# Regrouping sparse attention between feed-forward matmuls: two units of a set go through each stage together

## The chip, the cores and the metric

The kernel runs on one core of a Trainium2 chip. The core has five engines with instruction streams of their own: TensorE (PE in the profile, its weight loads PEld), VectorE (DVE), ScalarE (ACT), GpSimd (POOL) and SyncE (SP), which here issues DMAs. The metric is the device time of one execution in microseconds; lower is better. The median of three runs of the kernel before is 798.16 us (796.6 to 800.87).

## The reference

Block-sparse attention over 4 batches, 8 heads, 768 positions of 64 elements, followed by a feed-forward layer over all 3072 tokens. A query block of 32 positions sees its own key block and both neighbours, the first and the last block, and three sampled blocks; the first and the last query block see everything.

```python
scores = scale * np.matmul(q, k.transpose(0, 1, 3, 2))
mask = np.abs(blk_i - blk_j) <= window
mask = mask | (blk_i == 0) | (blk_j == 0) | (blk_i == n_blocks - 1) | (blk_j == n_blocks - 1)
...
scores = np.where(mask, scores, -1000000000.0)
scores = scores - np.max(scores, axis=-1, keepdims=True)
attn = np.exp(scores)
attn = attn / (np.sum(attn, axis=-1, keepdims=True) + 1e-09)
return np.matmul(attn, v).astype(np.float32)
...
h = x @ w_in
g = np.maximum(h, 0.0) + np.log1p(np.exp(-np.abs(h)))
return (g @ w_out).astype(np.float32)
```

Here x is the attention output with the heads side by side (512 columns), w_in is 512 x 2048, w_out 2048 x 512. Inputs and outputs are float32; the weights arrive as 64-bit words and are brought into float32 on the chip.

## The kernel before

**Attention.** A *set* is a batch and a group of four query blocks, with only the allowed key blocks (a sparse set), or the first and last query block of a batch against all keys (a *whole* set). A batch has seven sets: five sparse ones, the whole one, and one more sparse one of half the size; there are 28 in all. A set has two *units*, each with half of the heads. A unit goes through these functions:

- `scores` (line 606): matmuls into two PSUM banks (line 649 for sparse sets, 624 for the half-size one; 673 for the whole one, which takes two banks for each half of the keys, four in all), then on DVE a masked reduction that writes the scores to SBUF and their extremum (lines 655, 629, 680). For a sparse set these are four reductions.
- `exponents` (690): the exponential on ACT with its row sums (705), four per sparse unit.
- `transposes` (709): eight PE transposes of a sparse unit (718), four to a bank, so two banks; each bank is copied to SBUF by ACT (725) or DVE (723). In a set's first unit one copy goes to each of the two engines, in its second both go to ACT.
- `values` (730): small matmuls of the transposed weights with the values (761, 748, 775), all of a set into one bank of a pool of its own.

A set is ended by `normalise` (782, on DVE), `turn` (798: four PE transposes into one bank, tile y), `x_high` (817, ACT) and `x_low` (821, DVE). The last two read that bank and write the two parts of the feed-forward's input, and `x_low` of every third group stores them to DRAM.

**The feed-forward.** Each product of float32 matrices is made of three matmuls of high and low parts. In the first phase a *step* j treats one block of 128 hidden columns for a tile of 384 tokens: eight tiles by six blocks, 48 steps. In `first_half(j)` (292) stands `hidden` (248): twelve matmuls into one bank (lines 255 to 257, tile h), then ACT's absolute value and exponential (259, 260). In `second_half(j)` (297) stand `rounding` (263: 266 on ACT, 268 and 269 on DVE; 269 is the last reader of h's bank) and `project(j - 3)` (302): nine matmuls into three accumulators (313 to 315, tile o). ACT and DVE work of neighbouring steps (274, 279, 283, 289) completes the softplus. A second phase, after step 48, does the other ten blocks of hidden columns with tiles of 512 tokens and has no attention in it.

**PSUM.** Eight banks: three for o, one for x, and four of tag "s" (line 105), which h, s, t and y share.

**The order.** `pieces(n)` (828) makes three pieces out of unit n: `score_piece` (scores of unit n + 2), `value_piece` (exponents of n + 2, values of n) and `transpose_piece` (transposes of n + 1), with the ends of sets between them. 174 pieces stand in the list `attention` (918). `needs` (920) says how many must be done before the tile t of the feed-forward can start, and `due(x)` (950) spreads them evenly over the steps. The loop over j (973) emits `first_half(j)`, then pieces while fewer than `due(j + 0.5)` are done, then `second_half(j)`, then pieces up to `due(j + 1.0)`. In the steps 6 to 11, 18 to 23 and 30 to 35 this is three pieces, one unit, to a step; in the others about four. 22 pieces come before step 0. Pieces end at step 41.

`attend()` (924) runs one piece, then one `gather()` (477), which issues one waiting part of the key gathering (516 on DVE, 530 on POOL) and one of the value gathering (588, an indirect DMA on POOL), and one `convert()` (934), which advances the conversion of the weights (lines 160 to 206). Keys for the next group but one are requested by `load_keys` behind the second scores of a set, values by `load_values` behind its second values, queries by `load_queries` there too; the whole keys of the next batch are loaded (448) behind the last scores that read the old ones.

SP issues in the order of the program. On the other engines a planner at build time sets the order: it prefers the order of the program, and puts an instruction whose operands it takes to be ready ahead of one that has to wait. Instructions marked `keep_in_program_order` stay behind what precedes them on their engine.

## Time and profile before

| | us |
|---|---|
| median of three runs | 798.16 (796.6 to 800.87) |
| the profiled execution, its own time | 799.29 |
| its span in the profile | 797.5 |
| DVE e (268) waiting for ACT u (266), in total | 178.8 |
| ACT e (259) waiting for PE h (257), in total | 130.9 |
| POOL vg (588) waiting for PE x (761), in total | 38.6 |

The span runs from the first to the last instruction that the profiler saw; the profiled execution's time has 1.8 us more around it. Durations of single instructions come from that one execution. A matmul's row holds its whole passage through the array, and the rows of neighbours overlap; how far apart two rows start says what one costs. The page's chain of waits puts 66% of the span on PE, 16% on DVE and 11% on ACT. Most of the long totals in the table are idle time of engines that have nothing to do yet.

### The profile page before, as it was taken

To read this page: it belongs to the slowest core of one execution; us is meant where nothing else is said; L and a number is where in the kernel's file an instruction comes from. 1 tells how busy PE (TensorE), PEld (TensorE's weight loads), DVE (VectorE), ACT (ScalarE), POOL (GpSimd) and SP (SyncE) were. 2 spreads that over 40 slices of the span, in tenths; PEclk is the share of its full clock that TensorE was granted. 3 is DMA by queue.
4 is the path that set the end of the run, shared out by engine and by line. 5 is a ranking of instruction groups with operands and counts; after the bars stand their busy time and mean duration, and the time that the engine had idled before them with its cause. 6 is when DMAs were issued, how large, how long until landed. Compare 5 with 4: busy or idle time off the path is not lost.

```text
span 797.5 us, 20516 instructions
## 1 busy us (share of the span) xinstructions
PE 768.4 (96%) x7828; PEld 605.4 (76%) x7828; DVE 528.9 (66%) x1231; ACT 528.3 (66%) x1174; POOL 216.4 (27%) x389
## 2 busy tenths in 40 slices
PE   9779989998999999999999999999999999999997
PEld 8556667876777776787788888888888888888886
DVE  6789899787767878785656774555554553644544
ACT  5978978776777776777657875555555555555552
POOL 6874867425455435552000000000000000000000
PEclk9999999998999999999999999999999999999999
DMA  8999997876895886966415940330321312300201
GB/s 248 280 247 316 245 272 206 262 247 204 230 308 180 274 280 175 264 174 208 140 42 186 339 162 1 105 107 1 119 92 37 125 50 95 117 1 2 105 1 53
DMA packets 59729, 129.58 MB, mean 162 GB/s; under 512 B 5552, under 2 KB 17968, under 8 KB 58608
## 3 DMA queue, kind: packets, MB, share of 16 engines
q1 hardware_dynamic: 53632, 109.79, 44.5%
q0 software_dynamic: 5712, 17.57, 7.9%
q8 instruction: 61, 1.00, 0.5%
q10 hardware_dynamic: 288, 0.93, 0.3%
q14 instruction: 36, 0.29, 0.1%
HBM read 97.85 MB, written 30.41 MB: 161 GB/s over the span
## 4 chain that ended last, share of the span: by engine, by line
PE 66%; DVE 16%; ACT 11%; DMA 4%; issue 2%; SPq 0%; ACTq 0%; DVEq 0%
PE o L313 10%; PE o L314 10%; PE o L315 10%; PE h L255 9%; PE h L256 9%; PE h L257 9%; ACT pr L705 4%; PE t L718 2%; DVE pr L655 2%; DVE kg L516 2%; DMA vg<-in_v_dram 2%; PE x L761 2%; PE s L649 2%; DVE e L268 2%; DVE wt L183 1%
## 5 line engine op out<-in xcount | busy, mean ns | idle before, releaser
L268 DVE SCALAR_TENSOR_TENSOR e<-u,e 128x512 f32<-128x512 f32 (+1 forms) x108 | 76.7, 711 | 178.9 <-ACT u L266 178.8
L255 PE MATMUL h<-x,w 128*128 128x512 f32 (+1 forms) x432 | 163.2, 378 | 1.7 <-DVE e L269 0.9
L256 PE MATMUL h<-x,w 128*128 128x512 f32 (+1 forms) x432 | 159.3, 369 | 0.0
L257 PE MATMUL h<-x,w 128*128 128x512 f32 (+1 forms) x432 | 159.1, 368 | 0.0
L313 PE MATMUL o<-w,gh 128*128 128x512 f32 x384 | 156.5, 408 | 0.0
L314 PE MATMUL o<-w,gh 128*128 128x512 f32 x384 | 153.8, 401 | 0.0
L315 PE MATMUL o<-w,gl 128*128 128x512 f32 x384 | 152.1, 396 | 0.0
L259 ACT ACTIVATE e<-h 128x512 f32<-128x512 f32 (+1 forms) x108 | 59.3, 549 | 131.2 <-PE h L257 130.9
L705 ACT ACTIVATE pr<-pr,nmax 128x256 f32<-128x256 f32 (+1 forms) x192 | 102.2, 534 | 24.3 <-DVE nmax L686 12.0
L588 POOL DMA_INDIRECT vg<-in_v_dram,ix x88 | 87.6, 995 | 71.2 <-PE x L761 38.6
L255 PEld LDWEIGHTS h<-x,w 128*128 128x128 f32 x432 | 81.1, 188 | 19.3 <-DVE nmax L680 2.2
L530 POOL COPY kg<-kT 128x128 f32 x252 | 83.8, 378 | 39.4 <-PE s L649 31.2
L313 PEld LDWEIGHTS o<-w,gh 128*128 128x128 f32 x384 | 72.6, 189 | 24.4 <-issue 8.4
L283 ACT CAST gh<-u 128x512 fp32r<-128x512 f32 (+1 forms) x108 | 61.5, 569 | 43.5 <-PE o L314 41.0
L257 PEld LDWEIGHTS h<-x,w 128*128 128x128 f32 x432 | 81.2, 188 | 10.7
L256 PEld LDWEIGHTS h<-x,w 128*128 128x128 f32 x432 | 81.3, 188 | 10.6
L314 PEld LDWEIGHTS o<-w,gh 128*128 128x128 f32 x384 | 72.8, 190 | 17.6 <-issue 2.0
L315 PEld LDWEIGHTS o<-w,gl 128*128 128x128 f32 x384 | 72.6, 189 | 17.6 <-issue 0.4
L274 ACT ACTIVATE u<-u 128x512 f32<-128x512 f32 (+1 forms) x108 | 62.9, 583 | 23.2 <-DVE e L268 22.9
L289 DVE TENSOR_TENSOR gl<-u,gh 128x512 fp32r<-128x512 f32 (+1 forms) x108 | 69.4, 642 | 5.6 <-ACT gh L283 5.6
L279 DVE TENSOR_TENSOR u<-u,e 128x512 f32<-128x512 f32 (+1 forms) x108 | 69.6, 644 | 3.0 <-ACT u L274 1.6
L718 PE MATMUL t<-ident,pr 128*128 128x128 f32 x448 | 63.1, 280 | 7.9 <-DVE x L823 4.8
(88 smaller groups left out, 1060.4 us busy)
## 6 DMA issues: line engine op xcount, KB each, us to landing
vg<-in_v_dram SPq DMA_DIRECT2D x19, 768.0 KB, 6.7
xD<-x SPq DMA_DIRECT2D x8, 1536.0 KB, 8.3
raw<-in_w_in_dram SPq DMA_DIRECT2D x16, 512.0 KB, 9.2
raw<-in_w_out_dram SPq DMA_DIRECT2D x16, 512.0 KB, 8.8
qc<-in_q_dram SPq DMA_DIRECT2D x24, 256.0 KB, 6.9
vg<-in_v_dram SPq DMA_DIRECT2D x12, 512.0 KB, 7.2
yD<-os SPq DMA_DIRECT2D x24, 256.0 KB, 2.4
x<-xD SPq DMA_DIRECT2D x4, 1536.0 KB, 8.6
```

Of the source, the lines that this page charges most:

```text
L255: nc.tensor.matmul(ph, wh[:, cols], hi[:, c], start=(c == 0), stop=False)
L256: nc.tensor.matmul(ph, wh[:, cols], lo[:, c], start=False, stop=False)
L257: nc.tensor.matmul(ph, wl[:, cols], hi[:, c], start=False, stop=(c == NC - 1))
L268: nc.vector.scalar_tensor_tensor(out=e, in0=u, scalar=-1.0, in1=e, op0=ALU.add, op1=ALU.subtract)
L279: nc.vector.tensor_tensor(out=l, in0=l, in1=e, op=ALU.add)
L313: nc.tensor.matmul(po[m], gh[:, cols], wh, start=first, stop=False)
L314: nc.tensor.matmul(po[m], gh[:, cols], wl, start=False, stop=False)
L315: nc.tensor.matmul(po[m], gl[:, cols], wh, start=False, stop=last)
L530: copy(out=kd[:, i, 1 + NR + s, :], in_=kT[b][:, bass.ds(x, 1), :].rearrange("p n f -> p (n f)"))
L588: nc.gpsimd.indirect_dma_start(out=vd[0 : 3 * BLOCK, 1, i, :], out_offset=None, in_=v, in_offset=bass.IndirectOffsetOnAxis(ap=ix[:, b, 4 * ...
L705: nc.scalar.activation(x, x, AF.Exp, bias=nmax[rows, r, j : j + 1], scale=-1.0, accum_out=rs[rows, h : h + 1])
L718: nc.tensor.transpose(ps[:, i, 0:rows], st["pr"][r][0:rows, c * P : (c + 1) * P], ident[0:rows, 0:rows])
```

## The change

From set number 3 on (`SINGLE`), pieces are made for a whole set instead of for a unit. `set_pieces(k)` gives, for a sparse set followed by a sparse set, three pieces of count two: `scores_first` (`x_high` and `x_low` of the set before, then the scores of both units of the next set, and its key requests), `values_both` (exponents of both units of the next set, values of both units of this one, then the loads of values and queries) and `transposes_next` (`normalise`, transposes of both units of the next set, then `turn` of this one). `turn` stands directly behind `normalise` of the same set, where it came a unit later before. Around a whole set the pieces are cut differently, and both of its scores stand in neighbouring pieces.

The list `attention` now holds pairs of a count and a piece; `attend` adds the count to `done`, one by one, with a `gather` and a `convert` for each. The first loop, between `hidden` and `project`, does not run a `scores_first` unless attention is behind by more than `SLACK`. There are 169 units of count in place of 174 pieces, and 20 in place of 22 before step 0.

```diff
+SLACK = 2
+
+SINGLE = 3
...
+    def keys_behind(m):
+        b, g, whole = sets[m]
+        if not whole:
+            load_keys(place[b, g] + 2)
+        elif b + 1 < B:
+
+            gathered(key_work, place[b, g])
+            for n_ in range(4):
+                load_kT(b + 1, n_)
+            load_keys()
+
+    def set_pieces(k):
+
+        last = len(sets) - 1
+        nxt = k + 1 if k < last else None
+        out_ = []
+
+        def scores_first():
+            if k == SINGLE:
+                turn(k - 1)
+                transposes(2 * k + 1)
+            x_high(k - 1)
+            x_low(k - 1)
+            if nxt is not None:
+                scores(2 * nxt)
+                if not sets[nxt][2]:
+                    scores(2 * nxt + 1)
+                    keys_behind(nxt)
+
+        def scores_second():
+            exponents(2 * nxt)
+            scores(2 * nxt + 1)
+            keys_behind(nxt)
+
+        def exponents_next():
+            if nxt is not None:
+                if not sets[nxt][2]:
+                    exponents(2 * nxt)
+                exponents(2 * nxt + 1)
+
+        def behind_values():
+            load_values(k + 2)
+            if nxt is not None and not sets[nxt][2]:
+                load_queries(place[sets[nxt][:2]] + 2)
+
+        def values_first():
+            values(2 * k)
+            transposes(2 * k + 1)
+
+        def values_second():
+            exponents_next()
+            values(2 * k + 1)
+            behind_values()
+
+        def values_both():
+            exponents_next()
+            values(2 * k)
+            values(2 * k + 1)
+            behind_values()
+
+        def transposes_next():
+            normalise(k)
+            if nxt is not None:
+                transposes(2 * nxt)
+                if not sets[nxt][2]:
+                    transposes(2 * nxt + 1)
+            turn(k)
+
+        def split_last():
+            x_high(k)
+            x_low(k)
+
+        if sets[k][2]:
+            out_ += [(1, values_first), (2, scores_first), (1, values_second)]
+        elif nxt is not None and sets[nxt][2]:
+            out_ += [(1, scores_first), (1, scores_second), (2, values_both)]
+        else:
+            out_ += [(2, scores_first), (2, values_both)]
+        out_.append((2, transposes_next))
+        if nxt is None:
+            out_.append((1, split_last))
+        return out_
...
-    attention = [piece for n in range(len(units) + 2) for piece in pieces(n)]
-
-    needs = [3 * sum(1 for m, a in units if place[sets[m][:2]] < (t + 1) * GROUPS) + 4 for t in range(NTB)]
-    needs[-1] = len(attention)
+    attention = [(1, piece) for n in range(2 * SINGLE) for piece in pieces(n)]
+    split_in = {m: 3 * (2 * m + 3) + 1 for m in range(SINGLE - 1)}
+    for k_ in range(SINGLE, len(sets)):
+        split_in[k_ - 1] = sum(c for c, _ in attention) + (3 if sets[k_][2] else 2)
+        attention += set_pieces(k_)
+
+    total = sum(c for c, _ in attention)
+    needs = [
+        split_in[max(m for m, x in enumerate(sets) if place[x[:2]] < (t + 1) * GROUPS)] for t in range(NTB - 1)
+    ] + [total]
     done = 0
 
     def attend():
         nonlocal done
-        attention[done]()
-        done += 1
-        gather()
-        convert()
+        cost, piece = attention.pop(0)
+        piece()
+        for _ in range(cost):
+            done += 1
+            gather()
+            convert()
...
-        while done < len(attention) and done < due(j + 0.5):
+        while attention and done < due(j + 0.5) and (
+            attention[0][1].__name__ != "scores_first" or done + SLACK < due(j + 0.5)
+        ):
             attend()
...
-        while done < len(attention) and done < due(j + 1.0):
+        while attention and done < due(j + 1.0):
             attend()
```

More of the change, by code (lines that the diff above doesn't have):

```diff
@@ L957, in due @@
             last, at = end, needs[t]
-        return len(attention)
+        return total
     def load_w2(f):
@@ L990, in sparse_attention_ffn @@
         second_half(j)
-        while done < len(attention) and done < due(j + 1.0):
+        while attention and done < due(j + 1.0):
             attend()
         convert()
-        if done == len(attention) and ahead is None:
+        if not attention and ahead is None:
             assert weights.done(), weights.at
```

## The prediction

> **What bounds the kernel now.** I read the page's head first, then the busy time by stage, then the instructions in order of time inside one stage. The head says that TensorE (PE) is nearly always busy:
>
> ```profile
> span 797.5 us, 20516 instructions
> PE 768.4 (96%) x7828; PEld 605.4 (76%) x7828; DVE 528.9 (66%) x1231; ACT 528.3 (66%) x1174; POOL 216.4 (27%) x389
> ```
>
> That average mixes stages, so I cut the span where step 0, 6, 12, 18, 24, 30 and 36 of the first phase begins, and where attention has run out (stretch, length, then busy us and count of PE, PEld, DVE, ACT, POOL, granted clock, DMA share, GB/s):
>
> ```profile
> 57.08:119.74 62.66, 57.13 (x862) 40.66 (x855) 58.92 (x149) 53.67 (x133) 40.55 (x66) 0.97 0.99 279
> 119.74:166.50 46.76, 46.42 (x765) 36.97 (x763) 39.43 (x107) 37.31 (x99) 25.64 (x38) 1.00 0.76 239
> 166.50:228.71 62.21, 58.12 (x813) 43.46 (x812) 48.03 (x125) 45.34 (x115) 29.60 (x62) 0.95 0.79 238
> 228.71:276.53 47.82, 46.92 (x764) 37.08 (x763) 36.75 (x103) 37.19 (x101) 24.33 (x36) 1.00 0.77 237
> 276.53:335.38 58.85, 56.01 (x812) 42.26 (x811) 47.04 (x121) 43.74 (x111) 29.59 (x62) 1.00 0.84 244
> 335.38:384.54 49.16, 48.97 (x781) 37.77 (x779) 37.06 (x104) 35.20 (x97) 20.21 (x33) 1.00 0.64 190
> 421.65:446.87 25.22, 25.22 (x128) 22.78 (x127) 19.48 (x37) 20.55 (x43) 0.00 (x0) 1.00 0.70 245
> ```
>
> Steps 0 to 5 are bound by VectorE (58.92 of 62.66 us, 94%). From step 6 PE is the bound (46.42 of 46.76), with DVE at 84% and ACT at 80%. From there on whatever shortens PE's stream shortens the kernel, unless DVE or ACT are then asked for something sooner than they can give it.
>
> Now PE's stream inside one step, in order of time (start, duration, engine, line, operation). h is `hidden`, s `scores`, o `project`, x `values`, t `transposes`:
>
> ```profile
> 228.73 0.42 PE L255 MATMUL h<-x,w 128*128 128x384 f32 x1
> ...
> 230.73 0.34 PE L257 MATMUL h<-x,w 128*128 128x384 f32 x1
> 230.99 1.09 PE L649 MATMUL s<-kg,qc 64*32 64x256 f32 x32
> 232.02 0.50 PE L313 MATMUL o<-w,gh 128*128 128x512 f32 x1
> 232.36 0.39 PE L314 MATMUL o<-w,gh 128*128 128x512 f32 x1
> 232.59 0.40 PE L315 MATMUL o<-w,gl 128*128 128x512 f32 x1
> ...
> 234.76 1.10 PE L761 MATMUL x<-vg,pt 128*32 128x64 f32 x64
> 235.79 1.09 PE L718 MATMUL t<-ident,pr 128*128 128x128 f32 x8
> ```
>
> and where later steps begin, the last two without attention:
>
> ```profile
> 244.12 0.42 PE L255 MATMUL h<-x,w 128*128 128x384 f32 x1
> 426.08 0.34 PE L255 MATMUL h<-x,w 128*128 128x384 f32 x1
> ...
> 430.30 0.34 PE L255 MATMUL h<-x,w 128*128 128x384 f32 x1
> ```
>
> Two steps with two units, which is one set, take 244.12 - 228.73 = 15.39 us. A step without attention takes 430.30 - 426.08 = 4.22. So a set costs PE 15.39 - 2 x 4.22 = 6.95 us. How much of that is work? Inside s, eight weight loads fall into each stretch of 0.21 to 0.22 us, one per matmul, so 32 are four such waves, 0.86 us; x and t take what their weight loads take:
>
> ```profile
> 231.23:231.45 0.22, 0.22 (x16) 0.15 (x8) 1.00 1.02 261
> 231.45:231.66 0.21, 0.21 (x16) 0.15 (x8) 1.00 0.76 215
> 234.76 0.94 PEld L761 LDWEIGHTS x<-vg,pt 128*32 128x32 f32 x64 [0.17 <-DMA qc<-in_q_dram]
> 235.79 0.86 PEld L718 LDWEIGHTS t<-ident,pr 128*128 128x128 f32 x8
> ```
>
> I take 0.86 + 0.90 + 0.86 = 2.62 per unit, and 0.43 for the four transposes of `turn` (half of the eight): 2 x 2.62 + 0.43 = 5.67. The other 6.95 - 5.67 = 1.28 us are borders between kinds of matmul. They can be seen singly: s begins 0.26 after the last h; the first o begins 1.03 after s although s is 0.86 of work; the first o takes 0.34 where the next takes 0.23. Before, two steps hold ten such borders (h-s, s-o, o-x, x-t, t-h, twice; `turn` stands in front of x): 0.13 each.
>
> **The change part by part.** From `due()` I worked out which piece falls into which half step. All seven needs shift by 2 (22 becomes 20, 46 becomes 44 and so on; 174 pieces become 169 units of count), so the pace by step and the end of attention (step 41) stay. In the steps with three units of count (6 to 11, 18 to 23, 30 to 35) two steps become: h, both t with y, o, both s | h, o, both x. Borders: h-t, y-o, o-s, s-h, o-x, x-h: six for ten.
>
> Gain: 4 x 0.13 = 0.51 us a set. Counted by islands of attention among h and o it is three for four at 1.28 / 4 = 0.32 each, so 0.32; both are bounds from the same rows, and I take 0.5, since it is the borders that show in the rows. Twenty sparse sets get paired scores (24 less the first four). Four of them fall before step 6, where DVE is the bound, and get nothing. 16 x 0.5 = **-8 us**.
>
> Loss 1, PSUM banks. Tag "s" has four. Both t take four, y a fifth, and in those nine sets h still holds one: six for four. The nearest sight is step 17, where h, one t (two banks) and s (two) want five (PE, then ACT, then DVE):
>
> ```profile
> 219.24 0.44 PE L255 MATMUL h<-x,w 128*128 128x384 f32 x1
> ...
> 221.43 1.03 PE L718 MATMUL t<-ident,pr 128*128 128x128 f32 x8
> 222.40 2.23 PE L649 MATMUL s<-kg,qc 64*32 64x256 f32 x32
> 224.56 0.49 PE L313 MATMUL o<-w,gh 128*128 128x512 f32 x1
> 222.94 1.05 ACT L725 COPY pt<-t 128x512 f32<-128x512 f32 x2
> 224.45 0.56 DVE L268 SCALAR_TENSOR_TENSOR e<-u,e 128x384 f32<-128x384 f32 x1 [3.09 <-ACT u L266]
> 225.04 0.56 DVE L269 SCALAR_TENSOR_TENSOR e<-h,e 128x384 f32<-128x384 f32 x1
> ```
>
> s lasts 2.16 us to the next o instead of 1.03: 1.13 us lost until the copy of t gives a bank back; h's own bank comes only with L269, 6.4 us after h began. In the new order the second t tile is copied by DVE beside ACT, so I expect the fourth t to wait about 0.6 us (first t done 2.7 us after h starts, two activations of h and one copy of 0.53 before the bank is free, against a demand at 3.4). The program order is only a preference: an instruction whose operands are ready may be put ahead, so an o can fill the wait. I take 0.35, ends 0 and 1.13: 9 x 0.35 = **+3 us**.
>
> Loss 2, whole sets. Their two scores now follow each other with four banks each, in three batches behind step 6. Reducing 256 columns goes at this pitch:
>
> ```profile
> 233.55 0.42 DVE L655 CUSTOM_DVE_ANT_1 pr<-s,mask 128x256 f32<-128x256 f32 x1
> 233.90 0.42 DVE L655 CUSTOM_DVE_ANT_1 pr<-s,mask 128x256 f32<-128x256 f32 x1
> ```
>
> 0.35 us, so 384 columns about 0.5 (estimate) and four of them 2 us: the second unit waits between 0 and 2 us. I take 0.5: **+1.5 us**.
>
> Gain 2: at steps 17 and 29 the crowding just shown goes, since h is now followed by o: about -1.1 each. What is late next there: the transposes one step on need eight exponents at 0.53 us each, 4.3 us:
>
> ```profile
> L705 ACT ACTIVATE pr<-pr,nmax 128x256 f32<-128x256 f32 (+1 forms) x192 | 102.2, 534 | 24.3 <-DVE nmax L686 12.0
> ```
>
> between the pair of scores and the pair of transposes, which there lie x (1.9) and h (2.1), 4 us, apart. That may give half of it back: **-2 us** kept over the three crowded stretches, ends -3.5 and +2.
>
> Costed at nothing: the DMAs. Value loads (L570 and L582 on SP, L588 on POOL) are issued behind the second unit of a set as before, and used one pair later instead of three units later, so they have more time. Query loads stand behind them on SP in the same order. Key gathering (L516 on DVE, L530 on POOL) follows the second score as before; it stands behind eight reductions instead of four, and its user is two pairs away. The weight conversion gets two ticks in a row after a piece of count two; same work, burstier. If DVE's cover of 16% is not enough, L516 and L183 stand before the reductions that h needs, and each is a wait of 0.7 to 1.1 us. The start: a value and an exponent of set 3 move behind the first h, which begins 1 to 2 us sooner, but into the stretch that DVE bounds: 0, ends -2 and 0.
>
> Sum against the profiled run's own 799.29 us: -8 + 3 + 1.5 - 2 = -5.5, about **793.8 us**. The median of the runs shown, 798.16, lies 1.1 below the profiled one, so a median may come out 1 us lower.
>
> **The rivals.**
>
> *The banks give it all back.* If each of the sixteen pairs waits 0.5 us somewhere (the fourth t, or h behind both s, which fill all four banks), the sum is 0 and the time stays at 798 to 800. For it: four banks, and pairs that want all of them. Against: no wait at all in steps 6 to 11 today. The same time comes out if the pairs are pulled apart again because one half is ready sooner, so that the change doesn't do what it says. Together 0.31.
>
> *Slower: h behind the pair of scores.* s, s, h want five banks, and h gets its bank only when DVE has done the first unit's two reductions. If DVE is then in anything else, PE stands, and h, the head of the long chain h, three activations, L268, L269, starts late and the next demand on the banks with it. Its price is the 1.13 us of step 17, once per pair: 16 x (1.13 - 0.5) = +10, 809 us; it decides when the wait per pair passes 0.5 us. For it: DVE at 84%, one copy or conversion is 0.7 us. Against: the reductions of the first unit can run while PE does the second's 0.86. 0.21. [...]
>
> *Faster: the long waits go as well.* The clock was 0.97 and 0.95 in two stretches: 0.03 x 62.66 + 0.05 x 62.21 = 5.0 us lost. In the second, this piece of the chain of waits stands beside POOL's copies:
>
> ```profile
> 187.74 5.88 DVE kg L516
> 187.23 4.33 POOL L530 COPY kg<-kT 128x128 f32 x18
> ```
>
> If coarser pieces move those copies apart and PE does not pause, the clock stays whole: 793.8 - 5 = 789, and 3 us more without the DVE stall: 786. Against: the batch change keeps its place, steps 12 to 14. 0.14. [...]
>
> **How the numbers follow.** Forecast 0.34, all given back 0.31, slower 0.21, long waits gone 0.14. A measurement of this kernel can tell 0.5%, 4 us. The forecast, 5.5 us, lies just beyond that, and its own range (gain a set 0.32 to 0.51, banks 0 to 1.13) runs from 787 to 801; nearly all of its chance counts as faster. Faster 0.47, same 0.32, slower 0.21. The range reaches from the fast rival to most of the slow one: 784 to 807.
>
> **What would show it.** Right: between steps 6 and 11 two steps take about 14.9 to 15.3 us instead of 15.39, with x64, x64 and s32, s32 adjacent on PE. Loss 1 right: waits of PE t on ACT or DVE copies behind h, a few tenths each. Wrong: h waiting on L655 by more than 0.5 us per pair, PE busy well under 98% from step 6 on, or steps 0 to 5 longer than 62.7 us because bursts on DVE cannot be carried.

## The result and the profile after

| | before | after |
|---|---|---|
| median, us | 799.21 (796.6 to 800.87, 4 runs) | 809.13 (808.15 to 809.94, 4 runs) |
| ratio, 95% interval | | 1.0127 [1.0094, 1.0159] |
| the profiled execution, own time / span, us | 799.29 / 797.5 | 808.85 / 807.1 |
| start of step 0, of step 6, us | 57.08, 119.74 | 59.37, 129.63 |
| from step 6 to the end, us | 677.76 | 677.47 |

The change makes the kernel slower by 10 us, 1.3%. The forecast was 793.8, the range 784 to 807; 809 is the number of the slow rival. In the profile of after, lines up to 877 have moved by 4: L259 is the former L255, L653 is L649, L659 is L655, L722 is L718, L765 is L761, L273 is L269, L827 is L823.

The head of the page of after, and the longest of TensorE's waits (us in total, times, longest):

```profile
PE 762.3 (94%) x7828; PEld 614.6 (76%) x7828; DVE 521.0 (65%) x1231; ACT 527.6 (65%) x1174; POOL 218.4 (27%) x389
```

```profile
PE h L259 <- DVE nmax L659: 10.4, 9, 2.2
```

TensorE is busy for 6 us less than before (762.3 against 768.4, with as many matmuls) and yet ends 10 us later. The first matmul of `hidden` waits nine times, 10.4 us in all, for the reduction of the scores.

The same cuts as before, at the steps 0, 6, 12, 18, 24 and 30 of after and where attention has run out (stretch, length, busy us and count of PE, PEld, DVE, ACT, POOL, granted clock, DMA share, GB/s):

```profile
59.37:129.63 70.26, 60.23 (x911) 44.74 (x911) 60.29 (x155) 55.16 (x141) 42.02 (x67) 0.85 0.83 246
129.63:178.61 48.98, 45.70 (x766) 37.54 (x762) 38.44 (x103) 37.20 (x101) 24.39 (x36) 1.00 0.72 228
178.61:234.52 55.91, 52.98 (x818) 42.10 (x811) 42.59 (x121) 41.69 (x102) 29.19 (x59) 1.00 0.86 256
234.52:283.63 49.11, 45.04 (x767) 37.58 (x763) 38.03 (x106) 39.04 (x109) 24.62 (x38) 1.00 0.78 232
283.63:343.94 60.31, 54.54 (x817) 43.56 (x811) 44.24 (x123) 44.29 (x110) 31.54 (x62) 0.97 0.81 241
343.94:435.52 91.58, 90.05 (x1303) 75.22 (x1300) 57.03 (x161) 61.68 (x155) 21.45 (x34) 0.98 0.46 143
```

Against 62.66, 46.76, 62.21, 47.82, 58.85 and 90.47 us before (the last is 49.16 + 41.31, steps 30 to 41) that is +7.6, +2.2, -6.3, +1.3, +1.5 and +1.1. So in this pair of profiles the whole loss lies ahead of step 6 (2.3 us before step 0, 7.6 in steps 0 to 5). Behind it, gains and losses cancel. 64 values have moved from ahead of step 0 into steps 0 to 5 (880 matmuls ahead of step 0 instead of 944), and yet step 0 begins later. VectorE, which filled 94% of steps 0 to 5 before, fills 86% of them now: with about the same work (60.29 us in 155 instructions against 58.92 in 149) it is made to wait.

**Behind step 6.** TensorE's matmuls of step 6 in after, in order of time:

```profile
131.84 1.47 PE L722 MATMUL t<-ident,pr 128*128 128x128 f32 x12
133.07 0.48 PE L317 MATMUL o<-w,gh 128*128 128x512 f32 x1
133.61 0.66 PE L722 MATMUL t<-ident,pr 128*128 128x128 f32 x4
...
136.51 2.70 PE L653 MATMUL s<-kg,qc 64*32 64x256 f32 x64
140.43 0.41 PE L259 MATMUL h<-x,w 128*128 128x384 f32 x1 [1.23 <-DVE nmax L659]
```

and VectorE's instructions in the same stretch:

```profile
135.55 1.45 DVE L174 TENSOR_SCALAR wt<-wt 128x512 f32<-128x512 f32 x1 [0.38 <-ACT wt L164]
...
138.90 0.69 DVE L187 SCALAR_TENSOR_TENSOR wt<-raw,wt 128x512 int32<-128x512 int32 x1
139.51 0.42 DVE L659 CUSTOM_DVE_ANT_1 pr<-s,mask 128x256 f32<-128x256 f32 x1
...
139.85 0.42 DVE L659 CUSTOM_DVE_ANT_1 pr<-s,mask 128x256 f32<-128x256 f32 x1
```

Two things are to be seen. The fourth tile of transposes comes later than the third, and one matmul of `project` fills the gap (t x12, o, t x4); that it lacks a bank is what the other two profiles of this kernel say, in which it waits 0.7 us for ACT's copy of a tile t. And the pair of scores, which starts at 136.51, finds VectorE in three conversions of weights (L174, L181, L187) and three other instructions until 139.51. Only after two reductions does h get its bank: 3.92 us from s to h. Where VectorE is free, at step 32, the same order runs without a stall:

```profile
361.35 0.44 PE L259 MATMUL h<-x,w 128*128 128x384 f32 x1
...
368.20 1.96 PE L653 MATMUL s<-kg,qc 64*32 64x256 f32 x64
370.31 0.41 PE L259 MATMUL h<-x,w 128*128 128x384 f32 x1 [0.15 <-PE s L653]
...
376.59 0.44 PE L259 MATMUL h<-x,w 128*128 128x384 f32 x1
```

Here s to h takes 2.11, and two steps 376.59 - 361.35 = 15.24 us, against 15.39 before.

**Ahead of step 6.** TensorE's waits in the steps 0 to 5 of after (us in total, times, longest):

```profile
PE s L653 <- DVE e L273: 3.3, 1, 3.3
PE h L259 <- DVE nmax L659: 2.2, 1, 2.2
PE s L628 <- POOL kg L534: 2.1, 1, 2.1
```

Before, the longest in that stretch was one of 3.0, and the next 0.7. The first of the new ones in TensorE's order of time:

```profile
119.41 1.48 PE L653 MATMUL s<-kg,qc 64*32 64x256 f32 x34
124.18 1.95 PE L653 MATMUL s<-kg,qc 64*32 64x256 f32 x30 [3.29 <-DVE e L273]
```

Half of the scores run, then the pair wants a bank that h still holds: L273, the last reader of h, stands on VectorE behind 4 us of weight conversion, softplus and `normalise`. The granted clock falls as well, to 0.50 from 123.00 to 129.63 (0.85 over the steps 0 to 5), and the 128 values then take 3.64 us, where they take 1.99 at step 33 at a whole clock.

The second of the waits is that of the first matmul of step 0, and so lies ahead of that step. TensorE and VectorE in after:

```profile
54.47 2.70 PE L653 MATMUL s<-kg,qc 64*32 64x256 f32 x64
59.40 0.41 PE L259 MATMUL h<-x,w 128*128 128x384 f32 x1 [2.22 <-DVE nmax L659]
56.31 0.43 DVE L174 TENSOR_SCALAR wt<-wt 128x512 f32<-128x512 f32 x1
56.77 1.80 DVE L181 TENSOR_SCALAR wt<-wt 128x512 int32<-128x512 int32 x1
58.49 0.41 DVE L659 CUSTOM_DVE_ANT_1 pr<-s,mask 128x256 f32<-128x256 f32 x1
```

and in the kernel "scores apart" below (chip 2), whose matmuls stand in the same order there:

```profile
54.72 2.70 PE L653 MATMUL s<-kg,qc 64*32 64x256 f32 x64
57.58 0.41 PE L259 MATMUL h<-x,w 128*128 128x384 f32 x1 [0.16 <-PE s L653]
56.65 0.42 DVE L659 CUSTOM_DVE_ANT_1 pr<-s,mask 128x256 f32<-128x256 f32 x1
```

In after, two conversions of weights stand on VectorE ahead of the reductions; there, the reductions come first. The second conversion takes 1.80 us, where the median of its line is 0.43: GpSimd's own part of the conversion (L191) runs from 56.97 to 58.27, and so it does from 135.38 to 136.70, beside the L174 of 1.45 us in step 6. No run moved L191 alone.

### The profile page after: what moved, and what is told of

Same layout as the page of the kernel before. It is cut to its first block, busy times and chain, and to the rows that moved or that the text cites. A ratio compares the mean times of both kernels' runs of the same rounds, so it can differ in the third digit from the quotient of the medians.

```text
span 807.1 us, 20545 instructions
## 1 busy us (share of the span) xinstructions
PE 762.3 (94%) x7828; PEld 614.6 (76%) x7828; DVE 521.0 (65%) x1231; ACT 527.6 (65%) x1174; POOL 218.4 (27%) x389
## 3 DMA queue, kind: packets, MB, share of 16 engines
q8 instruction: 62, 1.02, 0.5%
## 4 chain that ended last, share of the span: by engine, by line
PE 76%; ACT 9%; DVE 8%; issue 3%; DMA 2%; POOL 0%; SPq 0%; DVEq 0%; POOLq 0%; ACTq 0%
PE h L259 11%; PE h L260 11%; PE h L261 11%; PE o L318 10%; PE o L317 10%; PE o L319 10%; PE x L765 4%; ACT pr L709 2%; PE t L722 2%; PE s L653 2%; ACT pt L729 2%; PE s L677 2%; PE warm L980 2%; ACT e L263 1%; DVE pr L659 1%
## 5 line engine op out<-in xcount | busy, mean ns | idle before, releaser
L272 DVE SCALAR_TENSOR_TENSOR e<-u,e 128x512 f32<-128x512 f32 (+1 forms) x108 | 72.4, 670 | 178.1 <-ACT u L270 177.7
L259 PE MATMUL h<-x,w 128*128 128x512 f32 (+1 forms) x432 | 165.5, 383 | 11.2 <-DVE nmax L659 10.4
L260 PE MATMUL h<-x,w 128*128 128x512 f32 (+1 forms) x432 | 161.8, 375 | 0.0
L261 PE MATMUL h<-x,w 128*128 128x512 f32 (+1 forms) x432 | 161.4, 374 | 0.0
L259 PEld LDWEIGHTS h<-x,w 128*128 128x128 f32 x432 | 82.8, 192 | 33.6 <-PE s L653 10.1
L261 PEld LDWEIGHTS h<-x,w 128*128 128x128 f32 x432 | 83.2, 193 | 10.7
L260 PEld LDWEIGHTS h<-x,w 128*128 128x128 f32 x432 | 83.0, 192 | 10.5
L293 DVE TENSOR_TENSOR gl<-u,gh 128x512 fp32r<-128x512 f32 (+1 forms) x108 | 72.3, 669 | 5.0 <-ACT gh L287 5.0
L273 DVE SCALAR_TENSOR_TENSOR e<-h,e 128x512 f32<-128x512 f32 (+1 forms) x108 | 67.9, 629 | 2.6
```

Source lines behind the costliest of these rows:

```text
L259: nc.tensor.matmul(ph, wh[:, cols], hi[:, c], start=(c == 0), stop=False)
L260: nc.tensor.matmul(ph, wh[:, cols], lo[:, c], start=False, stop=False)
L261: nc.tensor.matmul(ph, wl[:, cols], hi[:, c], start=False, stop=(c == NC - 1))
L272: nc.vector.scalar_tensor_tensor(out=e, in0=u, scalar=-1.0, in1=e, op0=ALU.add, op1=ALU.subtract)
L293: nc.vector.tensor_tensor(out=gl, in0=l, in1=G[n].bitcast(F32), op=ALU.subtract)
```

## The experiments

All ratios are to the kernel before, run beside it on the same chip. On two chips (5 and 2 below) the kernel before took 800 us, as in the result; on three others (9, 1 and 3) it took 811 to 812. There almost everything came out level; the end of this part says what is known of the reason. So the first four runs are to be read beside the later ones.

**Sets 3 to 8 unit by unit** (chip 9).

```diff
-SINGLE = 3
+SINGLE = 9
```

> Sets 3 to 8 go unit by unit as before, pairs begin with set 9 (step 6 on). Theory A (the loss arises before step 6: pairs there make PE pause, the granted clock falls to half for some 20 us, and later gains and waits of pairs cancel): the start of step 6 comes about 10 us earlier than in the changed kernel, the mean clock is back near 0.99, time about 799. Theory B (every pair loses the same by waits behind its scores; the low clock is by the way): 14 of 20 pairs are left, so about 0.7 of the 10 us, time about 806.

0.9994 [0.997, 1.0017]: level.

**Scores apart.** The two scores of a set in separate pieces, except behind a whole set; values and transposes still in pairs (chip 9).

```diff
-                if not sets[nxt][2]:
+                if sets[k][2]:
                     scores(2 * nxt + 1)
...
-        elif nxt is not None and sets[nxt][2]:
+        elif nxt is not None:
             out_ += [(1, scores_first), (1, scores_second), (2, values_both)]
```

> Values and transposes stay in pairs, but the two scores of a set are pieces of their own again. Theory A (the four banks that a pair of scores takes at once meet a DVE queue that still holds other work): the waits behind s64 go (about 14 us summed over the trace) and most of the half clock before step 6 (8 us), one more island a set costs 20 x 0.3 = 6 us: about 793. Theory B (the pairs of transposes, or the doubled ticks of weight conversion, make the bursts): 805 or more.

0.9949 [0.9915, 0.9982]. Steps 6 to 11 take 46.9 us and steps 18 to 23 47.6, as before the change: the waits of h are nearly gone (1.5 us in two, 10.4 in nine in after). Steps 0 to 5 still take 71.8.

What the edit does is not the same everywhere. In the steps with three units of count the two scores then stand apart on TensorE, with matmuls of the feed-forward between them. In the steps 0 to 5, and in the other steps with about four units, they still follow each other directly or with some values between (64 in one row at 54.72 us above); what changes there is the order on the other engines.

**No conversion behind the scores.** The ticks of weight conversion behind `scores_first` are made up for behind the next pieces (chip 9).

```diff
+    late = 0
...
+            if piece.__name__ == "scores_first":
+                late += 1
+                continue
             convert()
+            if late:
+                late -= 1
+                convert()
```

> The changed kernel, but scores_first is followed by no weight conversion; its ticks are made up behind later pieces. Theory C (conversion work traced right around the pair of scores stands before x_low and the reductions on DVE): the waits behind s64 in steps 6 to 11 fall from 0.6 to 1.8 us to under 0.3, time 4 to 8 us shorter, 801 to 805. Theory A without C (any DVE work will do, the planner fills the queue anyway): within 2 us of 809.

0.9973 [0.9948, 0.9999]; steps 6 to 11 at 50.3, steps 0 to 5 at 70.3. The waits of h are 4.5 us in five, against 9.9 in nine in the next run, on the same chip. So the conversion is part of what stands in the way, and not all of it: behind step 6 waits of 0.6 to 1.5 us are left.

**Without the rule of SLACK** (chip 9).

```diff
-        while attention and done < due(j + 0.5) and (
-            attention[0][1].__name__ != "scores_first" or done + SLACK < due(j + 0.5)
-        ):
+        while attention and done < due(j + 0.5):
```

> The changed kernel without the rule that a pair of scores waits for the projection. If the bank that h holds behind hidden matters, the pairs of scores that now stand between h and o wait for L269 (about 4 us behind h's end): 1 us or more for each of some 9 pairs, 815 to 825. If the place does not matter: within 2 us of 809.

1.0018 [0.9984, 1.0052]: no effect that can be told.

**Both kernels again** (chip 5), with a second profile of the kernel before.

> The changed kernel once more, beside many runs of the kernel before on the same chip, since four runs of each gave 799 against 809 on one chip and the kernel before took 812 on another. Theory D (the start of the kernel, up to step 6, depends on the chip and hides the difference where the kernel before also pauses there): ratio between 0.995 and 1.005 where the kernel before takes over 808, about 1.01 where it takes about 800. Theory A (pairs cost a fixed 10 us): ratio 1.010 to 1.015 on any chip.

> The kernel before, for a profile on the same chip. Theory D: where it takes over 808, the time is lost before step 6 (step 6 later than at 125 us, against 119.7 in the first profile), with half clock there; steps 6 to 41 take the same 306 us within 3.

1.0167 [1.0144, 1.0191]: the loss is there again, and somewhat larger. In this pair of profiles step 6 begins at 127.14 instead of 119.26 us, 7.9 later, step 12 at 178.81 instead of 165.99, 12.8 later, and the span is 12.8 longer (807.9 against 795.1). In the first pair step 12 was 12.1 later (178.61 against 166.50). So in both the whole loss is there by step 12; how it divides at step 6 differs.

**Values apart.** `values_both` as two pieces, scores and transposes in pairs (chip 5).

```diff
...
-            out_ += [(2, scores_first), (2, values_both)]
+            out_ += [(2, scores_first), (1, values_one), (1, values_two)]
...
```

> Scores and transposes in pairs, the two values of a set as pieces of their own. Theory E (128 values in a row after 64 scores run through PE's instructions faster than they are fetched: the pause of 2.9 us inside the values of step 29): that pause and the half clock behind it go, 4 to 5 us less than the changed kernel, but one more island a set, 20 x 0.3 = 6 us: about the same time as the changed kernel, or 3 us more. If the pause stays, it is not the row of values that makes it.

1.0131 [1.0107, 1.0155], 2.9 us less than after beside it (809.38 against 812.31). On TensorE the values still stand in rows of 128 (at 143.95 and 175.87, for example). So the edit did not take them apart, and what their pairs cost was not measured. The pause in the values of step 29 is still there, 2.8 us.

**Sets 3 to 8 unit by unit and all scores apart**, the first two edits together (chip 5).

> Both of e1 and e2: sets 3 to 8 unit by unit, and from set 9 on values and transposes in pairs, scores apart. Theory A or D with waits behind the pair of scores: steps 0 to 5 as in the kernel before, steps 6 to 41 without waits behind scores and with 0.3 to 0.5 us less a set than before, 14 x 0.35 = 5 us: ratio to the kernel before 0.993 to 0.996. Theory B: 1.000 or more.

0.9967 [0.9953, 0.998]: the whole loss is gone and a little more: 0.3% less than the kernel before. But which of the two edits does it?

**The square** (chip 2): after, each of the two edits alone, and both, beside each other.

> The changed kernel once more, as one corner of a square whose other corners run beside it on the same chip: sets 3 to 8 taken as pairs or not, and the two scores of a set adjacent or apart. Theory A (two separate losses that add): 1.3 to 1.7% over the kernel before, as seen so far. Theory B (one loss, the scores): the same.

> Sets 3 to 8 unit by unit, later scores in pairs. Theory A (pairs in the stretch that VectorE bounds cost 7 us up to step 6, adjacent scores behind it cost about 6 more): steps 0 to 5 back at 62 to 64 us, steps 6 to 11 at 49 to 50, and half of the loss left: 1.005 to 1.009. Theory B (adjacent scores are the whole loss, wherever they are): 1.008 to 1.013, since three quarters of the pairs are left.

> All sets from set 3 on with values and transposes in pairs, scores always apart. Theory A: steps 0 to 5 still 68 to 72 us, steps 6 to 11 at 47, and half of the loss left: 1.005 to 1.009. Theory B: no loss left, 0.995 to 1.000, with steps 0 to 5 at 62 to 64 us.

> Both edits together. Theory A: both losses gone, 0.995 to 0.999, steps 0 to 5 at 63 us and steps 6 to 11 at 47. Theory B: the same as with scores apart alone.

| | sets 3 to 8 in pairs | sets 3 to 8 unit by unit |
|---|---|---|
| scores in one piece | 1.0128 [1.0106, 1.015], 809.8 us | 1.0004 [0.9989, 1.0018], 799.55 us |
| scores in two pieces | 0.9994 [0.9981, 1.0007], 799.58 us | 0.9969 [0.9952, 0.9985], 797.29 us |

Both theories fell. Each edit alone takes 10 us off, both together 12.5. Two losses that add would have left half with either edit; adjacent scores alone, at one price per set, would have left most of it in the right upper corner. So nearly 8 us need both at once: sets 3 to 8 in pairs, and the scores of a set in one piece. The windows say where: steps 0 to 5 and steps 6 to 11, first after, then unit by unit, then scores apart, then both, and last the kernel before on chip 5 (columns as above):

```profile
60.10:126.96 66.86, 56.42 (x911) 43.41 (x912) 60.44 (x151) 53.08 (x134) 39.22 (x62) 0.92 0.88 259
126.96:178.66 51.70, 47.51 (x770) 39.12 (x763) 40.50 (x108) 39.60 (x109) 25.97 (x42) 0.97 0.68 216
```

```profile
58.42:120.16 61.74, 56.46 (x862) 40.64 (x855) 58.82 (x149) 53.77 (x133) 40.48 (x66) 0.97 1.00 282
120.16:168.01 47.85, 45.34 (x757) 37.10 (x755) 38.51 (x108) 37.74 (x102) 25.58 (x37) 1.00 0.77 235
```

```profile
57.55:124.13 66.58, 56.97 (x911) 42.42 (x911) 59.02 (x155) 53.85 (x137) 41.00 (x65) 0.92 0.89 269
124.13:171.11 46.98, 46.31 (x771) 36.85 (x763) 37.26 (x106) 39.17 (x107) 24.19 (x39) 1.00 0.78 237
```

```profile
58.16:120.88 62.72, 56.61 (x855) 40.63 (x856) 59.11 (x148) 53.70 (x133) 41.24 (x66) 0.97 0.97 278
120.88:168.07 47.19, 45.68 (x757) 36.88 (x755) 38.41 (x108) 37.59 (x101) 23.59 (x36) 1.00 0.76 236
```

```profile
57.33:119.26 61.93, 56.98 (x862) 40.71 (x856) 58.90 (x149) 53.69 (x133) 40.49 (x66) 0.97 0.99 283
119.26:165.99 46.73, 46.42 (x764) 36.97 (x763) 39.39 (x107) 37.33 (x99) 25.59 (x38) 1.00 0.77 238
```

Read the second rows first, by where step 12 begins: 178.66, 168.01, 171.11, 168.07, and 165.99 before. With the scores in two pieces, pairs in the early sets cost 171.11 - 168.07 = 3.0 us; scores in one piece on top of them 178.66 - 171.11 = 7.6; scores in one piece in the later sets only cost nothing by then. From step 12 to the end of attention, at step 41, scores in one piece cost 257.12 - 253.09 = 4.0 us with sets 3 to 8 unit by unit, and 257.88 - 255.73 = 2.2 with these sets in pairs (the lengths of that stretch in the four profiles). Where a kernel has several profiles on such chips, its step 12 begins within 0.5 us of the same time (178.61, 178.81 and 178.66 for after; 168.07 and 168.51 with both edits), so the 7.6 and the 3.0 stand clear of the scatter. Later stretches of one kernel differ by up to 2.5 us (steps 12 to 17 before: 62.21 and 59.74), so the 4.0 and 2.2 do not.

Of the 7.6, 2.6 lie ahead of step 0 (60.10 against 57.55), 0.3 in steps 0 to 5 and 4.7 in steps 6 to 11. Ahead of step 0 the first matmul of `hidden` waits 2.6 us in this profile of after, and not in the other corners, for what was shown above at 2.2. In steps 6 to 11 it waits three times, 3.0 us, and the clock is 0.97. Two of the three waits stand behind sets that are in pairs in the right upper corner too, where waits of 0.3 and 1.0 us made step 12 no later. In steps 0 to 5 the pairs cost 3.9 us (66.58 against 62.72) with the scores in two pieces and 5.1 (66.86 against 61.74) with one. The wait of the scores on L273 is 2.6 us in after, 2.0 with the scores in two pieces, which stand together on TensorE at that place all the same, and is gone with sets 3 to 8 unit by unit, where they stand apart. So in these steps the share of the scores and that of the paired values and transposes were not separated.

**Which half of the early pairs?** Only the early scores in two pieces, or only the early scores in one piece, values and transposes in pieces of their own; on chips 1 and 3, with the kernel before beside them on chip 3.

```diff
+    def behind_turn(k):
+        return k + 1 < len(sets) and not sets[k + 1][2] and (k >= 9 or sets[k][2])
...
-                if not sets[nxt][2]:
+                if behind_turn(k):
                     scores(2 * nxt + 1)
...
-        elif nxt is not None and sets[nxt][2]:
+        elif nxt is not None and not behind_turn(k):
```

```diff
...
+            if k < 9:
+                out_ += [(2, scores_first), (1, values_one), (1, values_two)]
+                return out_ + [(1, transposes_one), (1, transposes_two)]
             out_ += [(2, scores_first), (2, values_both)]
```

> The changed kernel with the two scores of sets 4 to 9 apart; from set 10 on they are adjacent; values and transposes go in pairs from set 3 on. Theory A (the adjacent scores of the early sets cost 7 to 8 us, by step 12): steps 0 to 5 at 66 to 67 us, steps 6 to 11 at 47 to 48, 1.001 to 1.005 times the kernel before. Theory B (adjacent scores cost about the same per set anywhere): 1.006 to 1.010.

> The changed kernel with values and transposes of sets 3 to 8 unit by unit and their scores adjacent. Theory A (adjacent early scores alone carry it): 3 us less than the changed kernel, steps 0 to 5 at 64 us or more, 1.008 to 1.012. Theory C (early scores cost only when the transposes behind them come in pairs too): steps 0 to 5 at 62 to 63 us, 0.999 to 1.004.

> The changed kernel with the scores of sets 4 to 9 apart, again. Where the kernel before takes 800 us, theory A (adjacent early scores cost 7 to 8 us): 1.001 to 1.005; theory B (adjacent scores cost the same anywhere): 1.006 to 1.010. Where it takes 811 us: within 0.3% of it, as before.

> The changed kernel with values and transposes of sets 3 to 8 unit by unit and their scores adjacent, again. Where the kernel before takes 800 us, theory A (adjacent early scores alone carry it): 1.008 to 1.012; theory C (only together with paired transposes): 0.999 to 1.004. Where it takes 811 us: within 0.5% of it.

> The kernel before, with a profile. Where it takes 800 us: steps 0 to 5 at 62 to 63 us and the start at 57 to 58, as seen. Where it takes 811 us: if the chip's disturbance lies in the start, step 0 begins at 64 us or later, with pauses of 0.7 us inside the values, and steps 0 to 5 take 64 us or more at a lower clock; if it lies in PE's later stream, the stretch behind step 6 is longer than 678 us.

Early scores in two pieces: 1.0005 [0.998, 1.0031] and 0.9991 [0.9971, 1.0011]. Early scores in one piece, the rest of the early sets in pieces of their own: 1.0025 [1.0001, 1.0048] and 1.0018 [0.9993, 1.0043]. The medians stand 811.72 against 814.56 and 810.67 against 814.06: the second kernel is the slower one on both chips, by 2.8 and 3.4 us, with intervals that overlap. In the profiles step 12 begins at 177.56 against 183.25 on chip 3 (178.61 for the kernel before), but at 186.64 against 186.82 on chip 1. And the second edit does only part of what it says: on TensorE the values stay in rows of 128, and the transposes come apart only from step 6 on. On both chips the kernel before took 811 to 812 us. So whether the scores carry the 8 us without paired values and transposes was not measured.

What may hide the loss on such a chip is to be seen in the profile of the kernel before on chip 3: the windows to step 0 and of steps 0 to 5, and one of TensorE's rows of values just ahead of step 0.

```profile
0.00:66.31 66.31, 52.88 (x944) 38.59 (x944) 42.22 (x156) 43.64 (x114) 45.37 (x96) 0.90 0.86 242
66.31:130.63 64.32, 57.44 (x863) 41.89 (x856) 58.42 (x146) 52.53 (x130) 40.84 (x66) 0.94 0.86 250
```

```profile
59.42 0.34 PE L761 MATMUL x<-vg,pt 128*32 128x64 f32 x6 [0.29 <-issue]
```

Step 0 begins at 66.31 instead of 57.08 and step 6 at 130.63 instead of 119.74: the kernel before is already as late there as after is on a chip of 800 us (129.63). TensorE stops in the middle of its values and waits for nothing that the profile shows: 18 such stops in the whole trace, 9.4 us in all, where the two profiles of this kernel on chips of 800 us have none in the values. The profiles of the variants on chips 9 and 1 have them too (17, 9.3 us, in the first of them). What makes three of the five chips of the experiments do so in the first 70 us stays open. The changed kernel itself was not run on one of them, so that these stops hide its loss is argued and not shown.

**Where the instruction stream is cut.** The fourth corner of the square with 32 more of the matmuls that run at the start before any data is there (`WARM` 82 instead of 50, chip 1). In the profile of after the instruction queue q8 moved 62 packets, and TensorE ran 7828 matmuls and as many weight loads. If all these packets are TensorE's, that is about 253 instructions to a packet, an estimate, and 64 are a quarter of one. For it speaks that from 100 to 200 us 11 packets go with 2792 instructions of TensorE, and from 500 to 600 us 3 with 861.

> Sets 3 to 8 unit by unit and all scores apart (the fourth corner), with 32 more of the matmuls that run at the start before any data is there, 82 instead of 50: 64 instructions more on PE, which move each later cut of its stream by a quarter of a fetch. If the pause belongs to the cuts, it leaves the values of step 29 (another place, or none); if it belongs to the order of work there, it stays at 2.5 to 3 us. Time 0.993 to 1.000 of the kernel before.

1.0015 [0.9991, 1.0039], on a chip of 811 us, so the time says nothing. What the run was for is the pause in the values of step 29, told below among what was not expected.

## Why the prediction was wrong

The profiled execution was forecast to gain 5.5 us and lost 9.6. Of these 15.1 us, 9.9 lie ahead of step 6, which the sum took at nothing, and 5.2 behind it, where the whole gain of 5.5 was to be and 0.3 was found.

**What bounds the kernel**: right as far as it went. From step 6 TensorE, in steps 0 to 5 VectorE. But from "bound by VectorE" I concluded only that the four early sets get nothing. I did not ask what coarser pieces do to the engine that bounds, and so put these sets and the start at nothing. That is the first step that failed.

**The gain of 0.5 us a set and the 0.35 for the banks**: right as a net in steps 32 to 35. There, where nothing stalls, two steps take 15.24 instead of 15.39 us, a net gain of 0.15, where 0.51 - 0.35 = 0.16 was worked out; "14.9 to 15.3" held. The fourth t waits as named, and one o fills the gap. The term fails in steps 6 to 11 and 18 to 23, where 48.98 and 49.11 us stand instead of 46.76 and 47.82. With the scores in two pieces the waits go, but steps 6 to 11 are then no shorter than before either (46.98 and 47.19 in the square). That is the second step that failed: a gain that holds where nothing stalls was put down for all sixteen sets, and the waits that take it away stood only in a rival. Two smaller slips changed little: the weight loads of x take 0.94 in the row shown and not 0.90, so the borders are 1.20 us and not 1.28; and the bounds named for the forecast's own range give 790.6 to 803.9, not 787 to 801, so less of its chance counted as faster than was said.

**The slow rival, h behind the pair of scores**: its wait is real. Nine waits, 10.4 us, on the reduction L659, for the reason that it gave (VectorE is in a conversion or a copy), and nearly all go when the scores are in two pieces: steps 6 to 11 are back at 46.98. Its price of 1.13 us for each of 16 pairs is 18 us of waits; behind step 6 eight waits of 8.2 us were found, about its price in each, in half as many pairs. Behind step 6 these waits are paid for by gains elsewhere, so in the first pair of profiles they make no difference there, 677.47 against 677.76. So the rival's 809 is the time measured, but for only part of its reason: 9.9 us of the loss lie ahead of step 6 in the first pair of profiles and 7.9 of 12.8 in the second, and its price counted no pair of that stretch, though the wait of 2.2 us ahead of step 0 is of its kind. That the two numbers agree is in part luck. The range ended at 807 and so left out the number of a rival that had a chance of 0.21.

What one pair of scores costs is not the same everywhere: s to h is 2.11 us at step 32 and 3.92 at step 6, with the same 64 matmuls and, at step 6, a VectorE that is busy with other work until 139.51.

**The start, costed at nothing (ends -2 and 0), and the early sets at nothing**: this is the term that failed. Step 0 began 2.3 us later and steps 0 to 5 took 7.6 more. It was named as a sign of being wrong ("steps 0 to 5 longer than 62.7 us because bursts on DVE cannot be carried"), but it had no price and no place in the sum. In the square, by step 12, it is 3.0 us for the pairs of the early sets and 7.6 more when their scores are in one piece as well. At two places the way it works is shown. The first h of step 0 was to begin 1 to 2 us sooner; it waits 2.2 us for reductions that stand behind two conversions of weights, and the wait goes when the scores are in two pieces. In addition a stop in the scores at 49 us, for which the profile shows no reason, is 2.39 us instead of 1.44. In step 5 half of the scores stand 3.29 us for the bank that h holds, because L273, which frees it, is queued on VectorE; the wait is gone with these sets unit by unit. How much of the 10 us are such waits and how much is the lower clock (0.85 and 0.92, against 0.97) was not separated.

**"If DVE's cover of 16% is not enough ... a wait of 0.7 to 1.1 us"**: the right condition, and it came true, at 0.6 to 1.4 us behind step 6 and 2.2 ahead of step 0. It had no place in the sum. With the conversion moved by one piece about half of the waits were found, so it is not the conversion alone that stands in the way.

**Whole sets, +1.5**: right. TensorE spends 4.67, 4.96 and 3.78 us on the scores of the three whole sets behind step 6, waits included, where before they took 4.38, 3.96 and 3.94 in their pieces: 1.1 us more.

**The crowded steps, -2**: right, and larger. Steps 12 to 17 take 55.91 us instead of 62.21 (59.74 in the second profile of before), and 56.1 to 56.4 in all corners of the square. So the gain needs neither scores in one piece nor the early pairs; which part of the rest of the change gives it was not tried. Step 17, where it was placed, takes 8.57 us instead of 9.49, as forecast; most of the rest lies in steps 13 and 14 (8.10 and 10.07 us instead of 9.63 and 14.37, or 9.63 and 11.87 in the second profile), which had no term. Steps 24 to 29 take 60.31 us instead of 58.85, but a pause of 2.6 us that was not forecast falls into them; without it a gain of 1.1 would stand there.

**The rival by which the clock goes whole**: in steps 0 to 5 it went the other way, to 0.85. In steps 12 to 17 the clock is whole in after (1.00 against 0.95), but it is 1.00 in the second profile of before too; so of the 6.3 us gained there, 2.5 are not the change's doing. That the clock stays whole where TensorE does not pause was the author's assumption. Before, the clock is 0.50 from 107.75 to 111.00 and from 193.50 to 199.50 us, behind or in the two longest pauses of TensorE (2.95 and 3.20 us); no run shows that pauses alone set it.

## What to carry to other kernels

Coarser pieces save borders on the engine that issues them, here 0.15 us in two steps where nothing stalls, and ask the engine behind it for a burst. Before the change that engine, VectorE, was busy for 94% of steps 0 to 5, 84% of steps 6 to 11 and 77% of steps 18 to 23, which became longer, and for 75% of steps 30 to 35, in four of which the saving stood. So price the change stage by stage, above all where another engine is the bound. Leave apart the work whose banks the next step needs at once, and look at what stands in the queue of the engine that empties them. In this kernel pairs of values and transposes from set 9 on, with the scores in two pieces, were 0.9969 [0.9952, 0.9985] of the kernel before, where pairs everywhere were 1.0128.

Two edits that each take away a loss can look like two causes. Only the corner with both, run beside the others, showed that they share most of it. And an edit of the program's order need not take apart what it names: two of the edits here left the values in rows of 128 on TensorE, which only the profile told.

## What was not expected of the hardware

**A pause that goes with the place in TensorE's instruction stream.** The last values of step 29 in after, in TensorE's order of time, and the instruction queue in the 1.7 us from 340.8 (packets, MB, share):

```profile
337.24 1.96 PE L653 MATMUL s<-kg,qc 64*32 64x256 f32 x64
339.13 1.53 PE L765 MATMUL x<-vg,pt 128*32 128x64 f32 x93
343.26 0.75 PE L765 MATMUL x<-vg,pt 128*32 128x64 f32 x35 [2.59 <-issue]
...
344.39 0.34 PE L261 MATMUL h<-x,w 128*128 128x384 f32 x1
...
345.10 0.52 PE L261 MATMUL h<-x,w 128*128 128x384 f32 x1
```

```profile
q8 instruction: 1, 0.02, 3.9%
```

A row of 128 values is left after 93, TensorE waits for no semaphore, a packet of instructions arrives, and 2.6 us later the row goes on. The pause is at this row in all three profiles of after and in seven of its variants, though not in the one without SLACK, where the scores ahead of the values are held up by a wait; neither profile of the kernel before on a chip of 800 us has it. With 64 instructions more at the start of TensorE's stream it leaves step 29, while it stays there in two other kernels run beside it, and appears in the values of step 17:

```profile
239.04 1.43 PE L765 MATMUL x<-vg,pt 128*32 128x64 f32 x86
243.07 0.86 PE L765 MATMUL x<-vg,pt 128*32 128x64 f32 x42 [2.60 <-issue]
```

So it depends on the place in the stream, not on the work of step 29 alone. Both places are ones where 64 scores and 128 values follow each other with nothing between: 384 instructions with their weight loads, in 4.1 us at step 29 without the pause. At the 253 instructions to a packet estimated above, they are one packet and a half; the 62 packets hold 1.02 MB, about 16 KB each. The pause would fit a packet that comes later than it is wanted. That is the author's guess; no run shows when a packet is asked for.

**The clock after a short pause.** In the rows above, the matmuls of h go from 0.34 to 0.52 us some 1.4 us after the pause ends, and their starts from 0.17 to 0.32 apart; the granted clock from 344.60 to 348.00 is 0.51. So here 2.6 us without a matmul were followed by a half clock. In the same profile 3.29 us without one (120.89 to 124.18) go with 0.50 from 123.00 to 129.63, and 1.93 us (from 102.64) were followed by 0.51 from 105.75 to 109.25, while behind 2.39 us (from 47.01) and 2.11 us (from 90.32) the clock is 1.00, from 49.40 to 57.17 and from 92.43 to 102.64. The length of one pause does not tell it in this trace; what does was not measured.
